# Attention and a maxout layer on one core: batch 1's second product stage in seven block products, with its weights' sums made earlier

## The chip, the cores and the metric

The kernel runs on one core of a Trainium2 chip. The core has a matrix engine (TensorE, "PE" in the profile, with its weight loads as "PEld"), a vector engine (VectorE, "DVE"), a scalar engine (ScalarE, "ACT"), a third elementwise engine (GpSimd, "POOL") and a queue engine that issues transfers (SyncE, "SP"). Each works through its own list of instructions in order, and they wait for each other through semaphores. The metric is the time in microseconds (us) of one execution on the device.

## The reference

Causal attention in a window of 128 for 8 batches, 8 heads, 576 rows and 64 columns a head, with a bias linear in distance, and then a layer that takes the largest of three products and multiplies it by an output matrix:

```python
scores = np.where(mask, scale * q @ k.T + bias, -1e9)      # mask: 0 <= rel < 128
attn   = softmax(scores)                                   # per head
x      = (attn @ v) with the heads side by side            # 4608 x 512
h      = np.maximum(np.maximum(x @ w1, x @ w2), x @ w3)    # 512 -> 768
out    = h @ w_out                                         # 768 -> 512
```

Everything is 32-bit. The kernel makes an exact-enough product from three products on PE: each operand is cut into a high part and a remainder, and high by remainder, remainder by high and high by high are summed in one bank of PSUM.

## The kernel before

The eight batches go one behind the other. Work on a batch has an attention part (L430 scores, L459 and L471 the softmax, L490 its division, L498 turns, L518 and L522 masks on POOL, L565 products with v, L598/599 the sums into `xk`) and then two stages of the layer, which take most of PE's time. Stage 1 makes nine groups of 128 rows of `h`, each from `x` and one of w1, w2, w3; stage 2 makes four groups of 128 rows of the output from `h`.

Each product of matrices is done on 2 by 2 blocks. In batches 0 and 1 ("plain", L773) it has eight block products, in two halves: stage 2 takes eight blocks of 18 matmuls, 144 in all. From batch 2 on (L825) it is done with seven block products, which need differences of the blocks on both sides: stage 2 takes 14 units of 9 matmuls, 126 in all. On the side of the weights the differences (called sums here) are made once; on the side of the data they are made per batch, by `factors_h` for stage 2: DVE makes four differences (L616), and seven factors are cut, each by an ACT cast (L612) and a DVE subtraction (L613). The plain way cuts four blocks and makes no difference.

The seven products of a group are added up in three banks of PSUM. The units come in the order k = 0, 1, 6, 2, 3, 4, 5, where k = 6 belongs to the group before. Unit 2 adds to the bank that unit 0 began, so it waits until unit 0's result has been copied out by ACT (L842); unit 3 does the same with unit 1's bank. At a plain stage there are only whole blocks, each begins a bank of its own, and three banks go round.

Weights' sums are made in the background, during batch 1 and the beginning of batch 2 (`more_sums`, called once for each unit of the layer): a load from DRAM by SP (`load_sums`, L230), four additions on POOL for each group (`sums`, L194, 128x256 each), a cut by two ACT casts (L199) and two DVE subtractions (L202), and a store by SP (`store_sums`). Groups 0 to 8 are stage 1's weights, and go back to DRAM, from where POOL's queue loads them into a ring for each batch (L361, L366). Groups 9 to 11 are stage 2's weights and stay on the chip in `ow`. They share one pair of buffers (`hs2`), each holding the rows of two groups. Before, groups are taken in the order 0 to 11.

A list of events with times sets the order of the program. PE's list is fixed by it; the other engines' lists are put in order by a scheduler, which places each instruction where its own model of time has it ready. SP's and POOL's transfers stand where the program has them. The order of each engine is shown below where it matters.

## Time and profile before

| | us |
|---|---|
| median of three runs (756.89 to 758.78) | 757.24 |
| the profiled execution | 755.7 |
| its span, first to last instruction | 754.0 |
| PE busy in it | 735.8 |
| DVE busy | 516.1 |
| ACT busy | 481.5 |
| POOL busy | 235.2 |

The granted clock of PE is at its upper level (1.0) over nearly the whole span. Times of instructions below count from the first instruction, so they are compared with the span; the execution's own time lies 1.7 us above it. Batch 1's layer begins at 161 us, its second stage at 235 us, and batch 2's layer at about 258 us.

### The profile page before, as it was taken

The numbers are of one execution on the slowest core, as the hardware profiler recorded it, in microseconds if no ns is written. First come the engines' busy times: TensorE is split into PE (matmuls) and PEld (weight loads), VectorE is DVE, ScalarE is ACT, GpSimd is POOL, SyncE is SP. The second block draws the span as 40 slices with busy tenths as digits, with TensorE's granted clock in tenths as the row PEclk, the third lists the DMA queues.
The fourth block names the chain that finished last, engine by engine and source line by source line (L and its number), as shares of the span: only waits on it lengthen the run. The fifth ranks groups of instructions, "written<-read, shape, count | busy, mean of one in ns | idle before, by whom it ended". The sixth has DMA issues, their size and how long they took to land.

```text
span 754.0 us, 19290 instructions
## 1 busy us (share of the span) xinstructions
PE 735.8 (98%) x7216; PEld 674.7 (89%) x7221; DVE 516.1 (68%) x1617; ACT 481.5 (64%) x1597; POOL 235.2 (31%) x451
## 2 busy tenths in 40 slices
PE   7979998999999999999999999999999999999998
PEld 3448897999999999999999999999999999999998
DVE  5869977636659567785678667794777747683663
ACT  5775677666667767776766757676666766552342
POOL 4651215545557123312222123221222122343100
PEclk9999999999999999999999999999999999999999
DMA  7867899759999289855988378864997468889711
GB/s 251 308 233 280 299 357 328 259 191 337 350 348 316 91 289 298 279 198 172 318 301 283 128 256 300 302 216 146 306 309 263 155 236 279 266 264 356 238 62 63
DMA packets 57085, 192.81 MB, mean 256 GB/s; under 512 B 5792, under 2 KB 24480, under 8 KB 50464
## 3 DMA queue, kind: packets, MB, share of 16 engines
q0 software_dynamic: 20304, 108.54, 43.3%
q1 hardware_dynamic: 36400, 82.85, 31.2%
q8 instruction: 57, 0.93, 0.5%
q14 instruction: 36, 0.29, 0.1%
q10 hardware_dynamic: 288, 0.20, 0.1%
HBM read 156.95 MB, written 34.60 MB: 254 GB/s over the span
## 4 chain that ended last, share of the span: by engine, by line
PE 77%; DVE 11%; ACT 6%; POOL 3%; issue 3%; DVEq 0%; ACTq 0%; POOLq 0%
PE ps_m L825 45%; PE ps_m L773 17%; PE ps_s L430 5%; PE ps_x L565 4%; PE pt L498 4%; DVE hs L613 2%; ACT p L471 2%; DVE hq L730 2%; DVE t L729 2%; POOL p L485 1%; ACT p L490 1%; POOL pp L522 1%; PE pt L374 1%; DVE t L616 1%; POOL pp L518 1%
## 5 line engine op out<-in xcount | busy, mean ns | idle before, releaser
L825 PE MATMUL ps_m<-xs,ring 128*128 128x288 f32 x2160 | 302.7, 297 | 0.6
L825 PEld LDWEIGHTS ps_m<-xs,ring 128*128 128x128 f32 x2160 | 290.1, 188 | 3.7 <-ACT t L842 3.2
L518 POOL TENSOR_SCALAR_AFFINE_SELECT pp<-pr 128x256 f32<-128x256 f32 x112 | 52.1, 465 | 281.4 <-ACT pr L502 155.8
L471 ACT ACTIVATE p<-s,st 128x128 f32<-128x128 f32 x288 | 114.7, 401 | 24.8 <-DVE st L459 22.6
L773 PE MATMUL ps_m<-xs,ring 128*128 128x288 f32 x864 | 122.5, 298 | 0.9 <-DVE hq L787 0.5
L842 ACT COPY t<-ps_m 128x288 f32<-128x288 f32 x196 | 76.7, 393 | 71.7 <-PE ps_m L825 69.7
L773 PEld LDWEIGHTS ps_m<-xs,ring 128*128 128x128 f32 x864 | 116.0, 188 | 3.6 <-issue 1.7
L366 POOL DMA_DIRECT2D ring<-keep x103 | 55.3, 537 | 166.0 <-PE ps_m L825 158.3
L825 PE MATMUL ps_m<-hs,ow 128*128 128x288 f32 x756 | 105.8, 297 | 0.4
L825 PEld LDWEIGHTS ps_m<-hs,ow 128*128 128x128 f32 x756 | 100.9, 188 | 2.7 <-ACT t L842 1.2
L490 ACT ACTIVATE p<-p,st 128x128 f32<-128x128 f32 x252 | 84.5, 393 | 22.2 <-DVE st L478 22.2
L729 DVE TENSOR_TENSOR t<-ps_m,t 128x288 f32<-128x288 f32 x108 | 48.8, 452 | 42.9 <-PE ps_m L825 32.5
L459 DVE CUSTOM_DVE_ANT_0 s<-ps_s,bias 128x128 f32<-128x128 f32 x240 | 60.9, 285 | 11.9 <-POOL bias L119 4.7
L430 PE MATMUL ps_s<-qk 64*64 64x192 f32 (+1 forms) x1088 | 61.4, 317 | 2.0 <-DVE st L459 1.3
L612 ACT CAST hs<-hq 128x288 fp32r<-128x288 f32 x96 | 40.4, 432 | 33.4 <-DVE hq L730 17.7
L471 ACT ACTIVATION_READ_ACCUMULATOR p<-s,st 128x1 f32 x288 | 55.3, 192 | 0.0
L565 PE MATMUL ps_x<-pp,v 64*64 64x64 f32 (+3 forms) x1456 | 53.4, 274 | 0.6 <-POOL pp L518 0.4
L498 PE MATMUL pt<-plus,p 128*128 128x128 f32 x288 | 48.7, 287 | 4.9 <-POOL p L485 4.4
L498 PEld LDWEIGHTS pt<-plus,p 128*128 128x128 f32 x288 | 30.4, 140 | 24.3 <-issue 11.5
L565 PEld LDWEIGHTS ps_x<-pp,v 64*64 64x64 f32 x1456 | 41.7, 133 | 11.0 <-issue 8.9
L730 DVE TENSOR_TENSOR hq<-t,hq 128x288 f32<-128x288 f32 x108 | 48.8, 456 | 2.1
L599 DVE TENSOR_TENSOR xk<-ps_x,xk 128x256 f32<-128x256 f32 (+3 forms) x56 | 25.4, 453 | 36.1 <-ACT xk L598 36.1
(92 smaller groups left out, 953.6 us busy)
## 6 DMA issues: line engine op xcount, KB each, us to landing
ring<-keep POOLq DMA_DIRECT2D x51, 1024.0 KB, 7.4
ring<-keep POOLq DMA_DIRECT2D x61, 768.0 KB, 6.0
qk<-in_qk SPq DMA_DIRECT2D x31, 576.0 KB, 5.6
hs<-in_w_all SPq DMA_DIRECT2D x12, 1023.6 KB, 7.0
v<-in_v SPq DMA_DIRECT2D x32, 320.0 KB, 6.6
outT<-t SPq DMA_DIRECT2D x64, 144.0 KB, 1.8
keep<-ring SPq DMA_DIRECT2D x9, 768.0 KB, 7.0
plain<-hs SPq DMA_DIRECT2D x12, 512.0 KB, 4.5
```

Source lines behind the costliest of these rows:

```text
L430: pe(nc.tensor.matmul(ps[j][d:d + D, o:o + k1 - k0], lhsT=qkt[u][j * D:(j + 1) * D, 0, q0:q0 + D], rhs=qkt[u][j * D:(j + 1) * D, 1, k0:k1] ...
L459: nc.vector.tensor_tensor_reduce(out=x, in0=ps[j][:, P:2 * P], in1=below, scale=-0.125, scalar=3.0e38, op0=ALU.add, op1=ALU.min, accum_out ...
L471: nc.scalar.activation(p[:, j], x, AF.Exp, bias=st[:, 0, a, j:j + 1], scale=-1.0, accum_out=st[:, 1, a, j:j + 1])
L490: nc.scalar.activation(p[:, j], p[:, j], AF.Copy, scale=st[:, 2, a, j:j + 1])
L498: pe(nc.tensor.transpose(out=pt[:, a, j], in_=p[:, j], identity=ident))
L518: nc.gpsimd.affine_select(out=old, in_=src, pattern=[[-x, n] for x, n in pat], compare_op=ALU.is_gt, fill=0.0, base=0, channel_multiplier=1,)
L565: pe(nc.tensor.matmul(x[j * D:(j + 1) * D, r, o:o + rhs.shape[1]], lhsT=vv[k, i, j * D:(j + 1) * D], rhs=rhs[k], start=start, stop=True, s ...
L729: nc.vector.tensor_tensor(out=s, in0=ps, in1=e, op=ALU.add)
L730: nc.vector.tensor_tensor(out=h, in0=s, in1=h, op=ALU.max)
L773: pe(nc.tensor.matmul(ps, lhsT=lt, rhs=rt, start=n == 0, stop=n == len(pairs) - 1, skip_group_check=True))
L825: pe(nc.tensor.matmul(part_of[n, {2: 0, 5: 0, 6: 0, 3: 1}.get(kk, kk)], lhsT=lt, rhs=rt, start=first, stop=i == len(pairs) - 1, skip_group ...
L842: nc.scalar.copy(out=e, in_=ps)
```

## The change

Batch 1's second stage takes seven block products, as the later batches do: the plain blocks of that stage are left out, and units 140 to 153 of the list take their place, 9 matmuls each (the last group's k = 6 follows in batch 2). For it, `factors_h` runs in batch 1's stage 1, and stage 1's last blocks come in the order (1,0), (0,0), (1,1), (0,1). The sums of stage 2's weights have to be there earlier, so groups 9, 10 and 11 come third to fifth; groups 7 and 8 come last, are loaded one at a time, and not before unit 156, that is, in batch 2. A group that is loaded alone uses the other half of its buffer for the high parts. The times after which a cut or a store may come are shortened by a unit.

```diff
--- before.py
+++ after.py
@@ -219,14 +219,18 @@
 
     now, loaded, finished = 0, 0, set()
     ts, to_sum, to_split = {}, [], []
+    sums_order = [0, 1, 9, 10, 11, 2, 3, 4, 5, 6, 7, 8]
 
     def load_sums():
         nonlocal loaded
         r = raw_tile()
-        for n in range(2):
-            g = loaded
+        single = loaded >= NG - 2
+        for n in range(1 if single else 2):
+            g = sums_order[loaded]
             loaded += 1
             ts[g] = t = r[:, 2 * DM * n:2 * DM * (n + 1)].rearrange("p (e w) -> p e w", e=4)
+            if single:
+                his[g] = r[:, 2 * DM:4 * DM].bitcast(F32R).rearrange("p (e w) -> p e w", e=4)
             nc.sync.dma_start(t.bitcast(F32), plain_keep[g])
             to_sum.extend((g, n, now + 8) for n in range(2))
 
@@ -238,7 +242,7 @@
             k, e = (slice(6, 7), slice(3, 4)) if a else (slice(1, 4), slice(0, 3))
             f = ow[:, k, g - 9]
             return hi_lo(f[:, :, 0], f[:, :, 1], t[:, e].bitcast(F32), True)
-        if a == 0:
+        if g not in his:
             x = xs_p.tile([P, 2, 2, C], F32R, name="xs")
             his[g] = x.rearrange("p a k c -> p (a k c)")[:, :2 * DM].rearrange("p (e w) -> p e w", e=4)
         e = slice(2 * a, 2 * a + 2)
@@ -251,8 +255,9 @@
         finished.add(g)
 
     def more_sums():
-        if loaded < NG and all(g in finished for g in range(loaded - 4, loaded - 2) if g >= 0):
-            load_sums()
+        if loaded < NG and all(g in finished for g in sums_order[max(0, loaded - 4):max(0, loaded - 2)]):
+            if loaded < NG - 2 or now >= 77 * PB + 2:
+                load_sums()
         if now < 63:
             return
         if to_split and now >= to_split[0][2] and (to_split[0][0] >= 9 or streamed > 2 * to_split[0][0] + 1):
@@ -260,14 +265,14 @@
             split_sums(g, a)
             if a:
                 if g < 9:
-                    later(now + 3, store_sums, g)
+                    later(now + 2, store_sums, g)
                 else:
                     finished.add(g)
         elif to_sum and now >= to_sum[0][2]:
             g, n, _ = to_sum.pop(0)
             sums(ts[g].bitcast(F32), n)
             if n:
-                to_split.extend((g, a, max(now + 6, 77 * PB if a and g >= 9 else 0)) for a in range(2))
+                to_split.extend((g, a, max(now + 5, 78 if a and g >= 9 else 0)) for a in range(2))
                 to_split.sort(key=lambda x: x[2])
 
     def place(n, a):
@@ -753,7 +758,7 @@
         if b == 0 and v == 1:
             spin(10)
         g, r = divmod(v, 4)
-        j, i = divmod(r, 2)
+        j, i = ((0, 0), (0, 1), (1, 0), (1, 1))[r] if b < PB - 1 else ((1, 0), (0, 0), (1, 1), (0, 1))[r]
         ps = ps_m.tile([P, 512], F32, name=f"ps_m{((PLAIN + 8) * b + v) % 3}")[:, :C]
         at = 9 * b + g
         if g < 9:
@@ -785,8 +790,10 @@
             return
         h = hq[p, (i, j)]
         nc.vector.tensor_tensor(out=h, in0=ps, in1=h, op=ALU.max)
-        if w == 2:
+        if w == 2 and b < PB - 1:
             later(unit_of(b, v + 1), plain_h, b, p, (i, j))
+        elif w == 2:
+            factors_h(b, p, (i, j), unit_of(b, v + 1))
 
     def unit(u):
         nonlocal now
@@ -795,7 +802,7 @@
         n, r = divmod(u, 7)
         k = (0, 1, 6, 2, 3, 4, 5)[r]
         n -= k == 6
-        if n < 11 * PB or n >= 11 * B:
+        if n < 11 * PB - 2 or n >= 11 * B:
             return
         if n == 11 * B - 1 and r > 4:
             k = 9 - k
@@ -830,7 +837,7 @@
         if g < 9:
             used.add((at, k))
         stream()
-        if b == PB and len(finished) < NG:
+        if len(finished) < NG:
             more_sums()
         if n == 11 * B - 2 and k < 2:
             for j in range(2 * k):
@@ -890,8 +897,13 @@
                     at(when, plain_x, b + 1)
                 else:
                     at(when, factors_x, b + 1, 77 * b + 63, 1.2)
-            at(when, plain, b, c)
-            when += pace if c < PLAIN else O_PACE * 14 / 8
+            if c < PLAIN or b < PB - 1:
+                at(when, plain, b, c)
+                when += pace if c < PLAIN else O_PACE * 14 / 8
+        if b == PB - 1:
+            for u in range(77 * b + 63, 77 * b + 77):
+                at(when, unit, u)
+                when += O_PACE
     for b in range(PB, B):
         pace = (ready[b + 1] - when) / 63 if b + 1 < B else O_PACE
         for u in range(77 * b, 77 * b + 77):
```

Three places show how instructions move.

On ACT, at the beginning of batch 1's layer (`hq<-ps_m` are copies of the first blocks out of PSUM, `xs<-hs` and `ow<-hs` casts of the sums), before:

```order
L199 CAST xs<-hs_1755 128x512 [waits DMAHW1_49,Pool_49]
L784 COPY hq<-ps_m_2339 128x288 [waits PE_49]
L490 ACTIVATE p<-p,st 128x128 [waits DVE_49]
L490 ACTIVATE p<-p,st 128x128 x3
L784 COPY hq<-ps_m_2364 128x288 [waits PE_49]
L199 CAST xs<-hs_1755 128x512
L199 CAST xs<-hs_1755 128x512 [waits DMAHW4_49,DMAHW5_49,DMAHW2_49,Pool_49]
L784 COPY hq<-ps_m_2392 128x288 [waits PE_49]
```

and in the changed kernel:

```order
L199 CAST ow<-hs_1755 128x256 [waits DMAHW1_49,Pool_49]
L495 ACTIVATE p<-p,st 128x128 [waits DVE_49]
L789 COPY hq<-ps_m_2343 128x288 [waits PE_49]
L495 ACTIVATE p<-p,st 128x128 x3
L199 CAST ow<-hs_1755 128x3x256 [waits DMAHW2_49,Pool_49]
L789 COPY hq<-ps_m_2367 128x288 [waits PE_49]
L199 CAST ow<-hs_1755 128x256
L789 COPY hq<-ps_m_2392 128x288 [waits PE_49]
L199 CAST ow<-hs_1755 128x3x256
```

The casts there are of stage 2's weights now, and the third of the copies (`ps_m_2367`) stands behind the cast of group 10's sums, which waits for POOL.

On POOL at the same place, before:

```order
L518 AFFINE_SELECT pp<-pr 128x2x128 [waits PE_49,Activation_49]
L522 AFFINE_SELECT pp<-pr 128x2x128 [waits PE_49]
L194 TENSOR_TENSOR hs_1755<-hs_1755 128x256 [waits DMAHW5_49,DMAHW1_49]
L194 TENSOR_TENSOR hs_1755<-hs_1755 128x256 [waits Pool_49]
L518 AFFINE_SELECT pp<-pr 128x2x128 [waits Activation_49]
L522 AFFINE_SELECT pp<-pr 128x2x128 [waits PE_49]
L518 AFFINE_SELECT pp<-pr 128x2x128
L522 AFFINE_SELECT pp<-pr 128x2x128 [waits PE_49]
L194 TENSOR_TENSOR hs_1755<-hs_1755 128x256 [waits Pool_49] x2
L194 TENSOR_TENSOR hs_1755<-hs_1755 128x256 [waits DMAHW2_49]
L194 TENSOR_TENSOR hs_1755<-hs_1755 128x256 [waits Pool_49]
L361 DMA ring<-keep_0_126 128x512 [waits DMASW0_49,PE_49]
```

and in the changed kernel:

```order
L523 AFFINE_SELECT pp<-pr 128x2x128 [waits Activation_49]
L527 AFFINE_SELECT pp<-pr 128x2x128 [waits PE_49]
L523 AFFINE_SELECT pp<-pr 128x2x128
L527 AFFINE_SELECT pp<-pr 128x2x128 [waits PE_49]
L194 TENSOR_TENSOR hs_1755<-hs_1755 128x256 [waits DMAHW5_49,DMAHW1_49]
L194 TENSOR_TENSOR hs_1755<-hs_1755 128x256 [waits Pool_49] x3
L194 TENSOR_TENSOR hs_1755<-hs_1755 128x256 [waits DMAHW2_49]
L366 DMA ring<-keep_0_126 128x512 [waits DMASW0_49,PE_49]
L194 TENSOR_TENSOR hs_1755<-hs_1755 128x256 [waits Pool_49] x3
```

The masks (AFFINE_SELECT) that stood between the sums come ahead of all of them, so eight additions and a ring load come in one piece.

On ACT, where batch 1's second stage begins (`hs` are factors of `h`, `xs` of `x`, `t<-ps_m` the copies of units 0, 1 and 2 or of a plain block), before:

```order
L490 ACTIVATE p<-p,st 128x128 x3
L612 CAST xs<-xt 128x576 [waits DMAHW6_49,DMAHW5_49,DVE_49]
L612 CAST hs<-hq 128x288 [waits DVE_49] x2
L598 COPY xk_3019<-ps_x 128x448 [waits PE_49]
L507 COPY pp<-pt 128x2x128 [waits PE_49,Pool_49]
L510 COPY pr<-pt 128x256
L612 CAST xs<-xt 128x576 [waits DVE_49]
L471 ACTIVATE p,st<-s,st 128x128 [waits DVE_49] x3
L713 COPY t<-ps_m_3481 128x288 [waits PE_49]
L471 ACTIVATE p,st<-s,st 128x128 [waits DVE_49]
```

and in the changed kernel:

```order
L617 CAST hs_3407<-hq 128x288 [waits DMAHW6_49,DMAHW3_49,DMAHW7_49,DMAHW2_49,DVE_49]
L617 CAST xs<-xt 128x576 [waits DMAHW7_49,DMAHW5_49]
L617 CAST hs_3407<-t_3399 128x288 [waits DVE_49]
L617 CAST hs_3407<-hq 128x288 [waits DVE_49]
L617 CAST hs_3407<-t_3400 128x288 [waits DVE_49]
L617 CAST hs_3496<-hq 128x288 [waits DMAHW4_49,DMAHW1_49,DMAHW5_49,DMAHW0_49,DVE_49]
L617 CAST hs_3496<-hq 128x288 [waits DVE_49]
L603 COPY xk_3026<-ps_x 128x448 [waits PE_49]
L617 CAST hs_3496<-t_3400 128x288 [waits DVE_49]
L512 COPY pp<-pt 128x2x128 [waits PE_49,Pool_49]
L515 COPY pr<-pt 128x256
L617 CAST xs<-xt 128x576 [waits DMAHW3_49,DMAHW2_49,DVE_49]
L849 COPY t<-ps_m_3504 128x288 [waits PE_49]
```

Seven casts of `h` and two of `x`, the second of which waits for DVE, stand ahead of the first copy of a unit's bank.

On PE at that place in the changed kernel (before, four blocks of 18 matmuls stood here, each in a bank of its own):

```order
L832 MATMUL ps_m_3504<-hs,ow 128x288 [waits DVE_49]
L832 MATMUL ps_m_3504<-hs,ow 128x288 x5
L832 MATMUL ps_m_3504<-hs_3407,ow 128x288 [waits DVE_49]
L832 MATMUL ps_m_3504<-hs_3407,ow 128x288 [waits Activation_49]
L832 MATMUL ps_m_3504<-hs_3407,ow 128x288
L832 MATMUL ps_m_3522<-hs,ow 128x288 [waits DVE_49]
L832 MATMUL ps_m_3522<-hs,ow 128x288 x5
L832 MATMUL ps_m_3522<-hs_3407,ow 128x288 [waits DVE_49]
L832 MATMUL ps_m_3522<-hs_3407,ow 128x288 [waits Activation_49]
L832 MATMUL ps_m_3522<-hs_3407,ow 128x288
L832 MATMUL ps_m_3504<-hs,ow 128x288 [waits Activation_49]
L832 MATMUL ps_m_3504<-hs,ow 128x288 x5
```

The third unit begins in the bank of the first (`ps_m_3504`), with a wait for ACT.

On POOL, in batch 2's first stage, before:

```order
L366 DMA ring<-keep_1_125 128x1536 [waits DMASW3_49,PE_49]
L366 DMA ring<-keep_0_126 128x2048 [waits DMASW5_49,PE_49]
L366 DMA ring<-keep_1_127 128x1536 [waits DMASW4_49,PE_49]
L518 AFFINE_SELECT pp<-pr 128x2x128 [waits Activation_49]
L522 AFFINE_SELECT pp<-pr 128x2x128 [waits PE_49,Pool_49]
L366 DMA ring<-keep_0_128 128x2048 [waits DMASW6_49,PE_49]
L366 DMA ring<-keep_1_129 128x1536 [waits DMAHW5_49,DMASW7_49,PE_49]
L366 DMA ring<-keep_0_130 128x2048 [waits DMASW0_49,PE_49]
```

and in the changed kernel:

```order
L371 DMA ring<-keep_1_125 128x1536 [waits DMAHW5_49,DMASW3_49,PE_49]
L194 TENSOR_TENSOR hs_3825<-hs_3825 128x256 [waits DMAHW4_49,DMAHW6_49,DMAHW3_49,DMAHW7_49,DMAHW2_49,DVE_49]
L371 DMA ring<-keep_0_126 128x2048 [waits DMASW5_49,PE_49]
L194 TENSOR_TENSOR hs_3825<-hs_3825 128x256 [waits Pool_49]
L371 DMA ring<-keep_1_127 128x1536 [waits DMAHW5_49,DMASW4_49,PE_49]
L194 TENSOR_TENSOR hs_3825<-hs_3825 128x256 [waits Pool_49] x2
L194 TENSOR_TENSOR hs_3840<-hs_3840 128x256 [waits DMAHW1_49,DMAHW5_49,DMAHW0_49,DVE_49]
L194 TENSOR_TENSOR hs_3840<-hs_3840 128x256 [waits Pool_49] x3
L371 DMA ring<-keep_0_128 128x2048 [waits DMASW6_49,PE_49]
L523 AFFINE_SELECT pp<-pr 128x2x128 [waits Activation_49]
```

The eight additions of groups 7 and 8 now stand between the loads of the ring.

## Rows read from the trace of the kernel before

**Rows 1.** the page, busy time of each engine: us, share of the span

```profile
PE 735.8 (98%) x7216; PEld 674.7 (89%) x7221; DVE 516.1 (68%) x1617; ACT 481.5 (64%) x1597; POOL 235.2 (31%) x451
```

**Rows 2.** windows of before, busy us of each engine in 20 us, then clock

```profile
220.00:240.00 20.00, 20.00 (x214) 19.18 (x213) 15.08 (x44) 13.94 (x47) 15.18 (x24) 1.00 1.00 334
240.00:260.00 20.00, 20.00 (x192) 19.20 (x191) 13.35 (x34) 14.82 (x47) 7.33 (x11) 1.00 0.42 146
```

**Rows 3.** list of waits from 140 us on: total us, times, longest

```profile
PEld ps_m L825 <- ACT t L842: 4.4, 16, 0.3
```

**Rows 4.** timeline of PE round batch 1's second stage: start us, us, line

```profile
226.69 6.62 PE L773 MATMUL ps_m<-xs,ring 128*128 128x288 f32 x48
...
235.35 9.69 PE L773 MATMUL ps_m<-hs,ow 128*128 128x288 f32 x72
...
246.19 9.77 PE L773 MATMUL ps_m<-hs,ow 128*128 128x288 f32 x72
```

**Rows 5.** timeline of POOL, 164 to 168 us

```profile
164.20 3.52 POOL L194 TENSOR_TENSOR hs<-hs 128x256 f32<-128x256 f32 x4
167.67 0.57 POOL L361 DMA_DIRECT2D ring<-keep  x1
```

**Rows 6.** one line's instructions, L194 on POOL: ns min/median/max, first and last start

```profile
L194 POOL TENSOR_TENSOR hs<-hs x48: 724/742/1251, 138.8 to 244.1; 128x256 f32<-128x256 f32 x48
```

**Rows 7.** timeline of ACT across the seam, 238 to 243 us

```profile
238.23 0.67 ACT L612 CAST xs<-xt 128x576 fp32r<-128x576 f32 x1 [1.88 <-DVE xt L616]
...
239.97 0.38 ACT L713 COPY t<-ps_m 128x288 f32<-128x288 f32 x1
...
242.65 0.83 ACT L199 CAST ow<-hs 128x768 fp32r<-128x768 f32 x1
```

**Rows 8.** timeline of ACT, 167 to 171 us

```profile
170.38 0.39 ACT L784 COPY hq<-ps_m 128x288 f32<-128x288 f32 x1
```

**Rows 9.** timeline of PE, 161 to 178 us

```profile
171.39 6.63 PE L773 MATMUL ps_m<-xs,ring 128*128 128x288 f32 x48
```

**Rows 10.** timeline of POOL, 238 to 278 us

```profile
238.44 6.79 POOL L194 TENSOR_TENSOR hs<-hs 128x256 f32<-128x256 f32 x6
...
273.19 0.53 POOL L366 DMA_DIRECT2D ring<-keep  x1 [3.35 <-PE ps_m L825]
...
277.12 0.55 POOL L366 DMA_DIRECT2D ring<-keep  x1
```

**Rows 11.** timeline of DVE across the seam, 231 to 245 us

```profile
233.72 0.81 DVE L787 TENSOR_TENSOR hq<-ps_m,hq 128x288 f32<-128x288 f32 x2
...
236.46 0.61 DVE L599 TENSOR_TENSOR xk<-ps_x,xk 128x448 f32<-128x448 f32 x1
...
237.32 0.87 DVE L616 TENSOR_TENSOR xt<-xk,xt 128x576 f32<-128x576 f32 x1
...
241.35 3.29 DVE L613 TENSOR_TENSOR xs<-xk,xs 128x576 fp32r<-128x576 f32 x3 [0.34 <-ACT xs L612]
```

**Rows 12.** one line's instructions, L613 on DVE, 250 to 400 us: ns min/median/max

```profile
L613 DVE TENSOR_TENSOR xs<-xk,xs x5: 742/745/853, 316.9 to 335.5; 128x576 fp32r<-128x576 f32 x5
```

**Rows 13.** groups of DVE and ACT instructions by form: busy us, mean ns

```profile
L613 DVE TENSOR_TENSOR hs<-hq,hs 128x288 fp32r<-128x288 f32 x96 | 44.1, 473 | 5.9 <-ACT hs L612 5.7
```

**Rows 14.** timeline of PE, PEld and ACT at the seam from batch 2 to 3

```profile
322.65 2.61 PE L825 MATMUL ps_m<-hs,ow 128*128 128x288 f32 x18
326.10 4.75 PEld L825 LDWEIGHTS ps_m<-hs,ow 128*128 128x128 f32 x36 [0.29 <-ACT t L842]
325.68 0.37 ACT L842 COPY t<-ps_m 128x288 f32<-128x288 f32 x1
```

**Rows 15.** DMA issues by form: KB each, median us from issue to landing

```profile
ring<-keep POOLq DMA_DIRECT2D x51, 1024.0 KB, 7.4
...
keep<-hs SPq DMA_DIRECT2D x9, 384.0 KB, 6.4
```

**Rows 16.** timeline of PE in batch 2

```profile
284.76 7.67 PE L825 MATMUL ps_m<-xs,ring 128*128 128x288 f32 x54
```

## The prediction

> **What bounds the kernel now.** I read the busy times first: PE is busy for 735.8 of 754.0 us, 98% [rows 1]. The windows say whether that holds at the place of the change: between 220 and 260 us PE is busy in all of it, at a granted clock of 1.00, with DVE at 13 to 15 us and ACT at 14 to 15 us in 20 [rows 2]. The list of waits then shows what little PE waits for: from 140 us on only the weight loads of the seven-product stages, which wait for ACT's copies 16 times, 4.4 us together and 0.3 at most [rows 3]. So fewer matmuls are worth their full time there, but only as long as the other engines keep PE supplied; there is no idle time of PE to give back, and each wait that the change makes is a loss of its own length. A measurement of this kernel can tell a change of about 0.3%, 2.3 us, from none.
>
> **What is removed.** Batch 1's second stage has 144 matmuls before (eight blocks of 18) and 126 afterwards (14 units of 9). The 72 matmuls of its first half take 9.69 us, those of the second 9.77 [rows 4]; by starts and ends that is 0.1346 us each, so 18 fewer give 18 x 0.1346 = 2.42 us. The last 9 of the 126 come in batch 2, which changes nothing in the sum. The gain as a whole is thus 0.32%, hardly more than a measurement can see, and every wait that is added counts against it.
>
> **Term A, the beginning of batch 1's layer.** The sums of groups 9 and 10 are made here in one piece: eight additions and a ring load on POOL, behind masks that end at 164.20 us. Four additions there take 3.52 us and the ring load's issue 0.57 [rows 5], so the piece takes between 8 x 0.742 + 0.57 = 6.5 us (by the median of the line [rows 6]) and 8 x 0.88 + 0.57 = 7.6: it ends between 170.7 and 171.8. ACT's cast of 128x768 waits for the last addition (0.83 us in [rows 7]), and the copy of `ps_m_2367` is queued behind it; the same copy ran at 170.38 at the latest before [rows 8]. With 0.05 us to start, some 0.75 for the cast and 0.39 for the copy, the bank is free between 171.9 and 173.0. PE wants it with the first matmul at 171.39 [rows 9]. That is a wait of 0.5 to 1.6 us; I take 1.0. The same pattern comes once more with group 11, whose additions have a ring load's issue in front of them: nothing to 0.57 us by that issue, taken as 0.3 (term B).
>
> Under these sums lies a question of contention. The additions on POOL take 742 ns in the median but 1251 at the most [rows 6]. Six of them beside large subtractions of DVE took 6.79 us, 1.13 each [rows 10], and three of these subtractions took 3.29 us, 1.10 each [rows 11], where the same form takes 0.745 when no additions run [rows 12]. So an addition and a subtraction cost each other about 0.35 us where they meet. The Trainium skill (SBUF — State Buffer, section "Who interferes with whom") states more: a VectorE operation with two SBUF inputs and a GpSimd operation that reads SBUF shut each other out for the whole operation. By that rule eight additions could hold DVE for 8 x 0.742 = 5.9 us; by the rows it is 8 x 0.35 = 2.8. The trace agrees in direction, and the price that I use is that of the rows.
>
> **Term C, the seam into batch 1's second stage.** This is the largest term. Unit 2 begins in unit 0's bank, so it waits for ACT's first copy. Units 0 and 1 are 18 matmuls, from 235.35 us to 235.35 + 2.42 = 237.77; that is when PE wants the copy. ACT has seven casts of `h` and two of `x` ahead of it, and the second cast of `x` waits for DVE's subtraction into `xt`. DVE's list is counted from the third block's maximum. Stage 1's last four blocks end 1.65 us apart, the last at 233.31 [rows 4], so that maximum runs from 231.75 to 232.15. Then come, at 0.4 us from start to start (two maxima take 0.81 us [rows 11]; a cut's subtraction is 0.473 in the mean [rows 13]): a subtraction of `x` (0.7), five operations of 288 columns, to 234.85; the last maximum and three more, 1.6; the sum into `xk`, 0.5 net of 0.61; one more cut, 0.4; a masked copy, 0.4; and the `xt` subtraction, 0.87 [rows 11]. That ends at about 238.6. Before, the same `xt` subtraction started at 237.32 and its cast on ACT waited 1.88 us for it and ran at 238.23, and the first copy at 239.97 [rows 7]; that hurt nothing, because plain blocks use three banks in turn. Now the cast begins at 238.65, the copy at about 239.35, and it ends at 239.75: PE waits 2.0 us.
>
> The nearest rows for a bound are those of a seam that has this form already. There PE begins at 322.65, the first copy starts at 325.68, 3.03 later, and six matmuls of unit k = 6 lie between, so that the wait is 0.29 [rows 14]. The copy's end there is 3.4 us behind the start of unit 0; without these six matmuls, as here, the wait would be 3.4 - 2.42 = 1.0. So C lies between 1.0 and, with DVE 0.5 us later, 2.5. Below nothing it can't be, since PE doesn't wait there now.
>
> What follows in that stage (two casts between the second copy and unit 3, the outputs' additions on DVE instead of copies on ACT) I cost at nothing: the wait at unit 2 lets ACT and DVE catch up. The buffers that the casts write were the sums' before, and SP's stores have to be done with them; a store takes 6.4 us in the median [rows 15] and is issued some 7 to 8 us ahead, so it is hidden by about 1 us, and if it isn't it takes part in the same wait.
>
> **Term D, batch 2's first stage.** The eight additions of groups 7 and 8 stand between ring loads on POOL. Six of them come behind the load that PE releases, 273.19 + 0.53 = 273.72 [rows 10]; at 0.86 each that is 278.9, where the next load of 1 MB was issued at 277.12 before [rows 10]. It lands 7.4 us later in the median [rows 15], at 286.3, and PE wants it six matmuls into the group that starts at 284.76, at 285.57 [rows 16]: 0.7 us late. With additions at 0.742 it is issued at 278.2 and lands in time; with 1.13 it is issued at 280.5 and is 2.3 us late. I take 0.7, from nothing to 2.3.
>
> **The sum.** -2.42 + 1.0 (A) + 0.3 (B) + 2.0 (C) + 0.7 (D) = +1.6 us on the profiled execution's 755.7, so 757.3 there. The median of the three runs shown is 757.24, 1.5 above the profiled one; a difference carries over, and the forecast is 757.24 + 1.6 = 758.8 us.
>
> **Rivals.**
>
> 1. Everything is hidden, and the gain shows in full: 757.24 - 2.42 = 754.8. For it: ACT and DVE idle for 32 and 36% of the span [rows 1], and the scheduler placed the copy where its own model of time had it ready. Against it: the order of ACT and DVE above leaves no room for the copy before 237.77. Slightly faster, at the edge of what can be seen.
> 2. The seam costs only what the regular one would (1.0), A its lower end (0.5), B and D nothing: 757.24 - 2.42 + 1.5 = 756.3. For it: the regular seam is measured, and my count of DVE's list is worth 0.5 us either way. Against it: the regular seam has fewer operations of DVE between.
> 3. Slower: POOL's additions in batch 2 run beside DVE's subtractions and take 1.13 us each, as they did at 238 us [rows 10]. The price is D's upper end of 2.3 from the late ring load, so 757.24 - 2.42 + 1.0 + 0.3 + 2.0 + 2.3 = 760.4, and up to 6 x 0.35 = 2.1 more, 762.5, if what DVE loses by it shows in PE's waits for banks. It decides against the change from the point where the load is issued after 285.57 - 7.4 = 278.2. For it: stage 1 of batch 2 has subtractions in it of the same sort. Against it: the median is 742 ns [rows 6], and DVE is less busy there than at the seam. The rule of the skill named above speaks for this case.
>
> **How the numbers follow.** The forecast's case has 0.34, and its own range, from the lower and upper ends of C and of half of A, is 757.5 to 759.7. Rival 1 has 0.21, rival 2 0.20, rival 3 0.25. Faster by over 0.3% (below 754.97) is rival 1, with 0.01 from rival 2: 0.22. Slower (above 759.5) is rival 3 and a quarter of the forecast's case: 0.33. The rest, 0.45, is within 0.3%. The range that leaves out 2 in 10 goes from rival 1's time, 754.8, to just below rival 3's upper price, 762.0.
>
> **What would show it.** In the changed profile the second stage of batch 1 should show 14 units of L832 where eight blocks of L773 stood. If C is right, the weight loads of L832 wait for ACT's copy once for about 2 us near 238 us, and that is the longest of PE's waits; if rival 2 is, for about 1; if rival 1 is, not at all. A shows as a wait of L778 for ACT's copy near 171 us, behind a cast that waits for POOL's L194; D as a wait of a weight load of batch 2's stage 1 for the ring near 285 us. The forecast is wrong if the windows from 160 to 300 us show PE busy in full as before, or if waits of more than 1 us show in places that are not named here, above all behind unit 3 in the second stage or at SP's stores.

## The result, and the profile after

| | before | changed |
|---|---|---|
| median | 756.89 us (5 runs, 755.21 to 758.78) | 766.55 us (5 runs, 765.42 to 768.58) |
| profiled execution | 755.7 | 768.58 |
| ratio | | 1.0131, interval 1.0114 to 1.0148 |

The change makes the kernel 1.3% slower, 9.7 us, well outside the range of the prediction. The page of the changed kernel, busy time of each engine, against [rows 1]:

```profile
PE 739.9 (96%) x7198; PEld 674.8 (88%) x7203; DVE 527.3 (69%) x1644; ACT 484.5 (63%) x1606; POOL 234.2 (31%) x451
```

DVE is busy for 11.2 us more, ACT for 3.0, PE for 4.1 although it has 18 matmuls less (its granted clock fell twice in this execution, as shown below). In the kernel before, PE's matmuls waited for nothing from 130 us on. In the changed kernel they have these waits (who waits for whom, us in total, times, longest):

```profile
PE ps_m L778 <- DVE hq L792: 2.2, 3, 1.4
PE ps_m L832 <- ACT t L849: 2.1, 1, 2.1
PE ps_m L832 <- DVE t L734: 1.9, 2, 1.1
PE ps_m L778 <- ACT hq L789: 1.2, 3, 0.8
PE ps_m L832 <- DMA ring<-keep: 0.6, 1, 0.6
```

Together that is 8.0 us. Four of the five are waits in the places of terms A and B (L778, stage 1 of batch 1) and D (L832 for DVE and for the ring); only the 2.1 us are at the seam. The timeline of PE shows where they stand (start, us, engine, line, count, idle time before it):

```profile
174.61 5.06 PE L778 MATMUL ps_m<-xs,ring 128*128 128x288 f32 x36 [0.17 <-ACT hq L789]
179.95 1.86 PE L778 MATMUL ps_m<-xs,ring 128*128 128x288 f32 x12 [0.27 <-DVE hq L792]
...
199.63 1.86 PE L778 MATMUL ps_m<-xs,ring 128*128 128x288 f32 x12 [0.81 <-ACT hq L789]
...
220.55 1.86 PE L778 MATMUL ps_m<-xs,ring 128*128 128x288 f32 x12 [1.42 <-DVE hq L792]
...
243.11 2.61 PE L832 MATMUL ps_m<-hs,ow 128*128 128x288 f32 x18
247.77 6.55 PE L832 MATMUL ps_m<-hs,ow 128*128 128x288 f32 x36 [2.06 <-ACT t L849]
...
288.49 1.07 PE L832 MATMUL ps_m<-xs,ring 128*128 128x288 f32 x6 [0.74 <-DVE t L734]
290.70 4.26 PE L832 MATMUL ps_m<-xs,ring 128*128 128x288 f32 x30 [1.15 <-DVE t L734]
...
298.33 6.91 PE L832 MATMUL ps_m<-xs,ring 128*128 128x288 f32 x48 [0.61 <-DMA ring<-keep]
```

PE's list is the same in both kernels but for the second stage. So its time can be taken apart by the distance from one group of products with v (L565 before, L570 now) to the next, from the timelines of the profiled executions:

| stretch (times of before) | before | changed | lost |
|---|---|---|---|
| 169.5 to 178.0 (term A) | 8.44 | 9.42 | 0.98 |
| 178.0 to 225.0 (term B) | 47.08 | 51.04 | 3.96 |
| 225.0 to 264.4 (second stage, with the nine matmuls in batch 2) | 39.32 | 40.82 | 1.50, where -2.42 was due: 3.92 |
| 264.4 to 301.7 (term D) | 37.35 | 40.91 | 3.56 |

Together that is 10.0 us; from 302 us to the end the two kernels agree within 0.1 us. The profiled execution also lost 2.8 us before 140 us, where PE's granted clock fell to 0.50 between 15 and 20 us. PE's list there is the same in both kernels, and the profiled execution without additions (below) does not lose it, so I count it to that one execution, which was 2.0 us above the median.

The seam, answering to [rows 7, 11], in ACT's and DVE's timelines:

```profile
246.75 0.67 ACT L617 CAST xs<-xt 128x576 fp32r<-128x576 f32 x1 [1.25 <-DVE xt L621]
247.33 0.39 ACT L849 COPY t<-ps_m 128x288 f32<-128x288 f32 x1
```

```profile
245.97 0.75 DVE L621 TENSOR_TENSOR xt<-xk,xt 128x576 f32<-128x576 f32 x1
```

The copy is behind the cast, and the cast behind the `xt` subtraction, as forecast; PE's wait is 2.06 us. What was not forecast stands in the next view, the windows round it (span; busy us and counts of PE, PEld, DVE, ACT, POOL; granted clock; DMA share; GB/s):

```profile
244.00:248.00 4.00, 1.94 (x15) 1.71 (x14) 3.90 (x14) 2.75 (x9) 1.36 (x2) 1.00 1.04 394
248.00:252.00 4.00, 4.00 (x22) 4.00 (x22) 2.30 (x7) 3.67 (x14) 0.00 (x0) 0.63 0.36 146
```

PE had stood still for two of four microseconds, and then the granted clock was 0.63 in the mean of the next four: the lower of the two levels (0.5) for most of it. The 36 matmuls behind the wait took 6.55 us; where the clock stayed up (below) they took 5.04.

### The profile page after: what moved, and what is told of

The parts are those of the page before. It is cut to its first block, busy times and chain, and to the rows that moved or that the text cites. A ratio compares the mean times of both kernels' runs of the same rounds, so it can differ in the third digit from the quotient of the medians.

```text
span 766.9 us, 19313 instructions
## 1 busy us (share of the span) xinstructions
PE 739.9 (96%) x7198; PEld 674.8 (88%) x7203; DVE 527.3 (69%) x1644; ACT 484.5 (63%) x1606; POOL 234.2 (31%) x451
## 4 chain that ended last, share of the span: by engine, by line
PE 64%; DVE 14%; ACT 8%; POOL 5%; DMA 3%; issue 3%; SPq 0%; DVEq 0%; ACTq 0%; POOLq 0%
PE ps_m L832 46%; PE ps_m L778 7%; PE ps_s L435 4%; PE pt L503 3%; PE ps_x L570 3%; DVE hs L618 3%; ACT p L476 2%; POOL hs L194 2%; DVE hq L735 2%; DVE t L734 2%; ACT p L495 1%; DVE t L621 1%; DMA qk<-in_qk 1%; DMA ring<-keep 1%; POOL pp L527 1%
## 5 line engine op out<-in xcount | busy, mean ns | idle before, releaser
L832 PE MATMUL ps_m<-xs,ring 128*128 128x288 f32 x2160 | 303.9, 297 | 3.2 <-DVE t L734 1.9
L832 PEld LDWEIGHTS ps_m<-xs,ring 128*128 128x128 f32 x2160 | 290.2, 188 | 7.3 <-ACT t L849 3.2
L476 ACT ACTIVATE p<-s,st 128x128 f32<-128x128 f32 x288 | 114.8, 401 | 25.5 <-DVE st L464 24.1
L778 PE MATMUL ps_m<-xs,ring 128*128 128x288 f32 x864 | 123.9, 299 | 4.3 <-DVE hq L792 2.7
L832 PE MATMUL ps_m<-hs,ow 128*128 128x288 f32 x882 | 124.9, 299 | 2.5 <-ACT t L849 2.1
L849 ACT COPY t<-ps_m 128x288 f32<-128x288 f32 x202 | 78.8, 393 | 75.1 <-PE ps_m L832 73.2
L832 PEld LDWEIGHTS ps_m<-hs,ow 128*128 128x128 f32 x882 | 119.3, 190 | 4.9 <-ACT t L849 3.5
L778 PEld LDWEIGHTS ps_m<-xs,ring 128*128 128x128 f32 x864 | 116.1, 188 | 8.4 <-DVE hq L792 3.5
L464 DVE CUSTOM_DVE_ANT_0 s<-ps_s,bias 128x128 f32<-128x128 f32 x240 | 61.0, 285 | 11.5 <-POOL bias L119 4.6
L476 ACT ACTIVATION_READ_ACCUMULATOR p<-s,st 128x1 f32 x288 | 55.4, 192 | 0.0
L570 PE MATMUL ps_x<-pp,v 64*64 64x64 f32 (+3 forms) x1456 | 53.5, 274 | 0.6 <-POOL pp L523 0.4
L735 DVE TENSOR_TENSOR hq<-t,hq 128x288 f32<-128x288 f32 x108 | 50.4, 471 | 2.1
L570 PEld LDWEIGHTS ps_x<-pp,v 64*64 64x64 f32 x1456 | 41.7, 133 | 11.0 <-issue 8.9
```

What stands on the lines that cost most here:

```text
L464: nc.vector.tensor_tensor_reduce(out=x, in0=ps[j][:, P:2 * P], in1=below, scale=-0.125, scalar=3.0e38, op0=ALU.add, op1=ALU.min, accum_out ...
L476: nc.scalar.activation(p[:, j], x, AF.Exp, bias=st[:, 0, a, j:j + 1], scale=-1.0, accum_out=st[:, 1, a, j:j + 1])
L570: pe(nc.tensor.matmul(x[j * D:(j + 1) * D, r, o:o + rhs.shape[1]], lhsT=vv[k, i, j * D:(j + 1) * D], rhs=rhs[k], start=start, stop=True, s ...
L735: nc.vector.tensor_tensor(out=h, in0=s, in1=h, op=ALU.max)
L778: pe(nc.tensor.matmul(ps, lhsT=lt, rhs=rt, start=n == 0, stop=n == len(pairs) - 1, skip_group_check=True))
L832: pe(nc.tensor.matmul(part_of[n, {2: 0, 5: 0, 6: 0, 3: 1}.get(kk, kk)], lhsT=lt, rhs=rt, start=first, stop=i == len(pairs) - 1, skip_group ...
```

## The experiments

All times are medians, and "less" is against the changed kernel's 766.55 us; the kernel before ran beside each set. Of each edit the lines that matter are shown, "..." marks where some are left out. The scheduler orders ACT's and DVE's lists anew for each edit, so these lists are not quite the same from run to run. The first question was which of two things made B and D so large: the extra work on factors, or POOL's additions.

**No additions.** `sums(ts[g], n)` is left out, so the sums are the plain blocks.

```diff
-            sums(ts[g].bitcast(F32), n)
```

> The changed kernel without POOL's additions of the background sums (L194), all of them; loads, casts, subtractions and stores stay. In the changed kernel's trace 4.0 us were lost between 193 and 234 us (waits for ACT's and DVE's maxima and copies), 1.0 at 172 us, 4.0 net at the second stage's start and 3.6 between 285 and 307 us. If the additions matter only where PE's wait comes behind them, the 1.0 at 172 us and the 3.6 in batch 2 go, and the rest stays: about 762. The rival is that additions and subtractions shut each other out all through batch 1, and that the 4.0 us come from that as well: then about 758. If they matter nowhere, 766.6.

It took 757.69 us (before beside it 756.65; ratio 1.0014, 0.9996 to 1.0032), 8.9 less than the changed kernel: the rival came true. Its page, and two of the three waits of PE from 130 us on (the third is 0.2 us):

```profile
PE 734.2 (97%) x7198; PEld 672.5 (89%) x7203; DVE 518.9 (69%) x1644; ACT 483.9 (64%) x1606; POOL 195.4 (26%) x403
```

```profile
PE ps_m L831 <- ACT t L848: 1.2, 1, 1.2
PE ps_m L831 <- DVE hq L734: 0.3, 1, 0.3
```

All waits of batch 1's stage 1 are gone, the distances there are those of before to 0.01 us (8.44, 10.07, 8.55, 9.96, 8.54, 9.97), and DVE, with the same instructions, is busy for 518.9 us instead of 527.3. The wait at the seam is 1.2 instead of 2.1, and batch 2's first stage still loses 0.7 us against before.

**Four cuts.** `factors_h` in batch 1 cuts the four blocks and makes no difference; units 4 to 6 read the factors of 0 to 2, so stage 2 of batch 1 is not the product. The additions stay.

```diff
...
+        if b < PB:
+            ks = {(0, 1): (3,), (0, 0): (0,), (1, 1): (2,), (1, 0): (1,)}[ij]
+            for k in ks:
+                later(when, cut, k, hq[p, ij])
...
```

> The changed kernel with four factors of h cut in batch 1 instead of seven, and without their four differences (units 4, 5 and 6 read the factors of 0, 1 and 2); PE's list is the same. If DVE's and ACT's extra work on factors makes the maxima late, the 4.0 us between 193 and 234 us go, and the wait for the first copy at the seam shrinks below 1 us, so that the clock does not fall: between 758.5 and 761. The rival, that the waits come from the sums in the background, gives 766 with at most the seam better (763).

It took 762.25 us, 4.3 less. PE's waits (one of 0.2 us is left out):

```profile
PE ps_m L844 <- DVE t L746: 2.7, 3, 1.2
PE ps_m L790 <- DVE hq L804: 0.6, 2, 0.3
PE ps_m L844 <- ACT t L861: 0.2, 1, 0.2
```

The wait at the seam is down to 0.2 us, and B to 0.6 us in one stretch (9.15 where before has 8.55). A stays (9.42), and batch 2 loses 5.0 us here instead of 3.56, because the clock fell there (0.8 between 280 and 288 us). So B needs both: it goes without the additions, and nearly goes without the extra work on factors.

**Filling the wait at the seam.** 16 matmuls into a bank of the turns, ahead of the unit that waits.

```diff
+        if u == 77 * (PB - 1) + 63 + 3:
+            fill = ps_t.tile([P, 512], F32, name="pt")[:, :C]
+            for i in range(16):
+                _, lt, rt = pairs[0]
+                pe(nc.tensor.matmul(fill, lhsT=lt, rhs=rt, start=i == 0, stop=i == 15, skip_group_check=True))
```

> The changed kernel with 16 more matmuls (2.15 us) on PE ahead of the unit that waits 2.06 us for the first copy, into a bank of the turns that nobody reads. If the granted clock falls because PE stands still there, and the 36 matmuls behind it took 6.55 instead of 4.98 us for that reason, the clock stays at 1.00 near 250 us and the time falls by about 1.6 us, to 765.0. If these matmuls were slow for another reason, the time stays at 766.6 or rises a little.

It took 767.27 us (four runs, 765.09 to 770.10): no gain. In its profiled execution the clock stayed up at the seam and fell later, in batch 2, behind D's waits (windows, clock third from the end):

```profile
248.00:252.00 4.00, 3.87 (x30) 3.64 (x29) 3.12 (x8) 3.43 (x12) 0.00 (x0) 1.00 0.34 141
280.00:300.00 20.00, 18.11 (x182) 16.72 (x183) 16.59 (x46) 12.85 (x41) 9.59 (x16) 0.91 1.02 353
```

So the fall is not tied to this one wait; by this one execution, filling moves it at most.

**The cuts of x later.** They are due four units later than in the changed kernel.

```diff
-                    at(when, factors_x, b + 1, 77 * b + 63, 1.2)
+                    at(when, factors_x, b + 1, 77 * b + 67, 1.2)
```

> The changed kernel with the cuts of batch 2's x due four units later, so that no cast of x stands ahead of the first copies on ACT. By the theory that the copy was late by ACT's order, PE's wait at the seam falls from 2.06 us to 0.5 or less, the clock stays up, and the time falls by 3 to 3.6 us, to 763. The rival is that the same work is late a moment later, at the first units of batch 2, which need these factors: then the wait moves there and the time stays within 1 us of 766.6.

It took 765.50 us, 1.0 less, which the intervals do not tell from the changed kernel (ratio 1.0088 to 1.0136 against 1.0114 to 1.0148), and the mechanism was missed. The wait is still 2.06 us, as PE's timeline shows, with ACT's behind it:

```profile
246.73 5.04 PE L832 MATMUL ps_m<-hs,ow 128*128 128x288 f32 x36 [2.06 <-ACT t L849]
```

```profile
241.96 0.77 ACT L617 CAST hs<-hq 128x288 fp32r<-128x288 f32 x2 [0.83 <-DMA keep<-hs]
...
245.51 0.40 ACT L476 ACTIVATE p<-s,st 128x128 f32<-128x128 f32 x1 [0.82 <-DVE st L464]
...
246.30 0.38 ACT L849 COPY t<-ps_m 128x288 f32<-128x288 f32 x1
```

With the casts of `x` away, the scheduler put the softmax's L476 ahead of the copy, and that waits for DVE too; before that, ACT's casts of `h` had waited 0.83 us for a store of the sums. The queue's next item took the place of the one removed. The 36 matmuls took 5.04 us here at a clock of 1.00: the same wait, without the fall.

**Memsets for additions.** Each addition is replaced by three memsets of the same piece, so the sums are zeros; they occupy POOL but read nothing.

```diff
+MEMSETS = 3
...
-            tc.keep_in_program_order(nc.gpsimd.tensor_tensor(out=t[:, to], in0=t[:, a], in1=t[:, b], op=op))
+            for _ in range(MEMSETS):
+                tc.keep_in_program_order(nc.gpsimd.memset(t[:, to], 0.0))
```

> The changed kernel with each of POOL's additions replaced by three memsets of the same 128x256 piece, which read nothing from SBUF (so the sums are zeros); POOL stays occupied and ACT's casts still wait for it. Without the additions the time fell to 757.7. If the additions hurt because their reads and DVE's subtractions shut each other out, the memsets do not hurt DVE: DVE's subtractions of 128x288 stay at 0.45 us and the waits between 193 and 234 us and near 290 us are gone, the wait near 172 us (ACT behind POOL) may stay: 757.5 to 759.5. If it is POOL's occupancy (casts and ring loads queued behind it), the time stays near 766.

It took 759.87 us (ratio to before 1.0030, 1.0013 to 1.0048), just above the range expected if the reads were what hurts. POOL's line (ns min/median/max):

```profile
L196 POOL MEMSET hs<- x144: 301/314/341, 140.1 to 290.6; 128x256 f32 x144
```

POOL is busy as long as in the changed kernel (233.9 against 234.2 us), and yet DVE is back at 518.8 us and stage 1 of batch 1 at before's distances (8.44, 10.07, 8.54, 9.96, 8.72, 9.96). DVE's subtractions of 128x288 take 0.46 us at most there (1.98 in the changed kernel, between 160 and 235 us). DVE's list is the same in stage 1 but for a few instructions that stand a place or two elsewhere. So what stretches DVE's instructions is not POOL's being busy but what its additions read. How much of B is this stretching is not shown by it: ACT's casts of the sums, too, wait less for POOL here (4.8 us in all between 160 and 306 us, 11.5 in the changed kernel), and some of them stand a few places later in ACT's list. For A this run proves still less: the copy stands ahead of the cast there. In batch 2, 1.1 us of waits for the ring remain (loads behind POOL's pieces), with 2.1 us lost between 264 and 302 us.

**Without the additions of groups 7 and 8**, the ones in batch 2, alone:

```diff
-            sums(ts[g].bitcast(F32), n)
+            if g not in (7, 8):
+                sums(ts[g].bitcast(F32), n)
```

> The changed kernel without the additions of groups 7 and 8 alone, the ones that stand in batch 2. By the reading of the trace they cost what batch 2's stage 1 lost between 275 and 307 us, 3.3 us less the 0.7 that stayed without any additions: the time falls by 2.6 us, to 764, and the waits between 193 and 234 us stay as they are. The rival, that batch 2's loss follows from the late second stage of batch 1 and not from its own additions, gives 766.5.

It took 762.64 us, 3.9 less where 2.6 was expected. Batch 2's loss falls from 3.56 to 1.1 us, and the rest of the difference is the clock, which did not fall at the seam in the profiled execution (the 36 matmuls behind the same wait took 4.99 us). B and A stay to 0.02 us. So the eight additions cost 2.5 us of D. The meeting is part of it: in the changed kernel DVE's subtractions of 128x512 there took 964 ns in the mean, here 680. It is not all of it, because memsets, which read nothing, left 2.1 us of loss there.

**Unit 4 third**, which puts 1.2 us between unit 1 and unit 2:

```diff
-        k = (0, 1, 6, 2, 3, 4, 5)[r]
+        k = ((0, 1, 6, 4, 2, 3, 5) if n == 11 * PB - 2 else (0, 1, 6, 2, 3, 4, 5))[r]
```

> The changed kernel with batch 1's first group in the order of units 0, 1, 4, 2, 3, 5: unit 4 begins a bank of its own and puts 9 matmuls (1.21 us) between unit 1 and unit 2, which waits for the copy. The wait of 2.06 us at the seam becomes 0.85, the second stage no longer lets PE stand still for 2 us, and the time falls by 1.2 us, or by up to 2.8 where the granted clock had fallen behind the wait: 764.5 at the middle. The rival: unit 4's own factor, the last one that is cut, is late, or a later unit waits instead, and the time stays at 766.5.

It took 764.86 us, 1.7 less, with the whole result; by the intervals that is no clear difference (1.0070 to 1.0124 against 1.0114 to 1.0148). The wait became 0.89, as expected, and unit 5 then waits 0.64:

```profile
241.84 3.79 PE L832 MATMUL ps_m<-hs,ow 128*128 128x288 f32 x27
246.51 2.63 PE L832 MATMUL ps_m<-hs,ow 128*128 128x288 f32 x18 [0.89 <-ACT t L849]
249.79 1.45 PE L832 MATMUL ps_m<-hs,ow 128*128 128x288 f32 x9 [0.64 <-ACT t L849]
```

In the profiled executions the stretch from the second stage to batch 2's first group takes 38.93 us, against 39.27 in the run with the cuts of `x` later, which has the old order and no fall of the clock either. So the order alone shows as 0.3 us; the rest of the 1.7 goes with the clock.

**No additions and unit 4 third.** This run has the edits of "No additions" and of "Unit 4 third" together.

> No additions at all and the unit order 0, 1, 4, 2, 3, 5 together. Without additions PE still waited 1.18 us at the seam; the unit order should take that away. If nothing else is in the way, the 18 matmuls now show: 757.7 less 1.2, 756.5, that is 0.3 below the kernel before, with 0.7 us still lost in batch 2's stage 1. If the gain of 2.4 us comes out whole it is 754.5; if the wait only moves on, it stays at 757.7.

It took 757.25 us (ratio 1.0010, 0.9995 to 1.0025), between the first and the last of its three expectations: one wait of 0.6 us is left at the seam, and 0.7 us for the ring in batch 2.

**Additions on DVE**, with unit 4 third, the whole result:

```diff
-            tc.keep_in_program_order(nc.gpsimd.tensor_tensor(out=t[:, to], in0=t[:, a], in1=t[:, b], op=op))
+            tc.keep_in_program_order(nc.vector.tensor_tensor(out=t[:, to], in0=t[:, a], in1=t[:, b], op=op))
```

> The unit order 0, 1, 4, 2, 3, 5 of the run before, with the additions made by DVE instead of POOL; it computes the whole result. Additions and subtractions then stand in one queue and cannot meet, ACT waits for no POOL, and the ring loads have nothing ahead of them; but DVE gets 48 additions of some 0.42 us, 20 us more work, where the meeting of the two cost DVE 8.4 us. By the theory that the meeting is what costs, it is faster than with POOL (764.9): about 760. If what counts is only how much DVE has to do in batch 1, it is slower: 768 or more.

It took 758.05 us (before beside it 757.67; ratio 1.0000, 0.9978 to 1.0023). The additions on DVE, and PE's waits from 130 us on:

```profile
L194 DVE TENSOR_TENSOR hs<-hs x48: 393/419/658, 141.4 to 273.3; 128x256 f32<-128x256 f32 x48
```

```profile
PE ps_m L832 <- DMA ring<-keep: 1.4, 1, 1.4
PE ps_m L832 <- ACT t L849: 1.2, 2, 0.6
```

DVE is busy for 535.4 us here, 8.1 more than in the changed kernel, and PE waits for 2.6 us in all instead of 8.0. Batch 1's stage 1 is at before's distances in all six stretches. That settles the rival "DVE has too much to do" for A and B. D is only in part better: batch 2's first stage still loses 2.0 us, 1.4 of them in the wait for the ring.

**The kernel before without the additions**, by the same edit as in "No additions", is the other corner:

> The kernel before without the additions of the background sums. If the additions cost time only together with the changed kernel's extra work on factors, since before PE waited for nothing from 140 us on, the time stays as before within 0.3%: 756 to 758. If they cost PE something in the kernel before too, it falls below 755.

It took 756.14 us against 757.67 beside it (ratio 0.9975, 0.9953 to 0.9997): 1.5 us less at the middle of an interval that begins at 0.2. In its trace the distances from 137 us on are before's to 0.07 us, and the first addition starts at 138.8 us. So the additions cost 8.9 us in the changed kernel, and by the medians 1.5 in the one before, which no wait or stretch of PE shows; where these would come from stays open. DVE is busy for 509.7 us here: the additions made its instructions 6.4 us longer in the kernel before as well (516.1), and the change's own work on DVE is 9.2 us (518.9 without additions).

**Sooner cuts and stores**, on top of additions on DVE and unit 4 third:

```diff
-                to_split.extend((g, a, max(now + 5, 78 if a and g >= 9 else 0)) for a in range(2))
+                to_split.extend((g, a, max(now + 2, 78 if a and g >= 9 else 0)) for a in range(2))
...
-                    later(now + 2, store_sums, g)
+                    later(now + 1, store_sums, g)
```

> The run before (additions on DVE, unit order 0, 1, 4, 2, 3, 5), with the sums' cuts due three units and the stores one unit sooner; the result is whole. In the run before PE still waited 1.2 us at the seam, where ACT's casts wait for a store of the sums, and 1.4 us near 294 us for a ring load that shares the DMA engines with the stores of the last two groups. If sooner stores take half of both away, the time falls by 1.2 us, to 756.8, at last below the kernel before (757.7) by some 0.1%. If the cuts on ACT and DVE only get in the way of other work, it stays at 758 or rises.

It took 763.62 us (before beside it 757.02), a miss. Its six runs lie between 759.35 and 765.08, and the one with a trace is the lowest: there 0.8 us is lost in batch 1's stage 1 again, and the waits at the seam are 1.8 in all. To what the other runs lost 3 to 6 us more, no trace shows; it stays open.

**Additions on DVE alone**, with the changed kernel's unit order:

> The changed kernel with one edit: the additions on DVE instead of POOL; the unit order is that of the changed kernel, and the result is whole. With both edits the time was 758.05, and the unit order alone was worth 1.7 us (766.55 to 764.86). If the meeting of additions and subtractions is the main cause, this one edit takes 7 us or more: 758.5 to 760. If the two edits worked only together, it stays above 763.

It took 759.56 us (ratio 1.0042, 1.0022 to 1.0061), 7.0 less than the changed kernel. The two longest of PE's waits:

```profile
PE ps_m L832 <- ACT t L849: 2.2, 1, 2.2
PE ps_m L832 <- DMA ring<-keep: 1.0, 1, 1.0
```

A and B are gone altogether (8.44 in A's stretch, and before's distances to 0.01 us in B's). The seam's wait stands as in the changed kernel, and the clock fell behind it here too (0.57 between 244 and 248 us; the 36 matmuls took 6.55 us). D is 1.6 us. No version of the changed kernel is faster than the kernel before: the best whole one is level with it.

## Why the prediction was wrong

The forecast was +1.6 us, and +9.7 came. Term by term:

- **The gain, right as far as it can be seen.** The 18 fewer matmuls were to give 2.42 us from the second stage to the first stretch of batch 2. In the run with four cuts, which waits least there (0.2 us), that stretch takes 37.53 us against 39.32, 1.8 less; some 0.4 us of the gain is not accounted for.
- **Term A, right in size, in part by luck.** It was 0.98 us against 1.0. The wait that was forecast, for the copy behind the cast that waits for POOL, is less than half of it: the first matmul came at 174.61 where the kernel before would have had it at 174.20 (171.39 [rows 9] and the 2.81 us by which the changed kernel is late here), so 0.4 us, below the range of 0.5 to 1.6. The other 0.6 is a wait for DVE's maximum (PE's row at 179.95 above). It was not forecast: DVE's list stood still for 6.81 us ahead of the subtraction that cuts the same sums and waits for ACT's casts of them, and the maximum behind it came late:

```profile
173.43 0.83 ACT L199 CAST ow<-hs 128x768 fp32r<-128x768 f32 x1 [3.42 <-POOL hs L194]
174.17 0.39 ACT L789 COPY hq<-ps_m 128x288 f32<-128x288 f32 x1
```

```profile
176.00 0.96 DVE L202 TENSOR_TENSOR ow<-hs,ow 128x768 fp32r<-128x768 f32 x1 [6.81 <-ACT ow L199]
...
179.44 0.45 DVE L792 TENSOR_TENSOR hq<-ps_m,hq 128x288 f32<-128x288 f32 x1
```

- **Term B, the step that failed.** It was taken as "the same pattern once more", one ring issue of 0.57 us at most, and priced at 0.3; the rest of stage 1 lost 3.96. The pattern itself cost nothing: ACT's casts of group 11's sums did wait 1.37 us for POOL, but the stretch in which they stand takes 10.07 us, as before:

```profile
188.39 1.14 ACT L199 CAST ow<-hs 128x768 fp32r<-128x768 f32 x2 [1.37 <-POOL hs L194]
```

The loss is in the four stretches behind it (1.07, 0.73, 1.67 and 0.48 us), which the forecast did not name; its own sign of being wrong, a wait of more than 1 us in an unnamed place, stands at 220.55 us. Two things were left out of its working. One is that stage 1 of batch 1, too, gets more work from the change: in the seam's count DVE's differences and extra cuts were all listed, but for the first two thirds of `h` they fall between 186 and 223 us, and nothing was reckoned there. The other is the meeting of additions and subtractions. [rows 6, 10, 11] had its price, about 0.35 us, and the forecast worked out 2.8 us for eight additions; but as a loss of DVE's time it stands in no term of the sum, and only in rival 3, for batch 2. The lines of the changed kernel round the longest of these waits, on POOL, DVE and ACT:

```profile
208.56 4.33 POOL L194 TENSOR_TENSOR hs<-hs 128x256 f32<-128x256 f32 x4
```

```profile
208.77 1.07 DVE L202 TENSOR_TENSOR hs<-hs,xs 128x512 fp32r<-128x512 f32 x1 [1.24 <-POOL pp L527]
...
220.04 0.45 DVE L792 TENSOR_TENSOR hq<-ps_m,hq 128x288 f32<-128x288 f32 x1
...
220.62 1.03 DVE L621 TENSOR_TENSOR t<-hq,t 128x288 f32<-128x288 f32 x1
221.57 0.99 DVE L618 TENSOR_TENSOR hs<-hq,hs 128x288 fp32r<-128x288 f32 x1
```

```profile
212.92 0.62 ACT L199 CAST xs<-hs 128x512 fp32r<-128x512 f32 x1 [1.84 <-POOL hs L194]
213.44 1.28 ACT L495 ACTIVATE p<-p,st 128x128 f32<-128x128 f32 x4
214.63 0.42 ACT L617 CAST hs<-hq 128x288 fp32r<-128x288 f32 x1
```

Four additions take 4.33 us instead of 2.97 (0.742 each [rows 6]). ACT's casts wait for them, and the softmax and the casts of `h` are queued behind these casts. DVE then has seven operations on factors and the scores to catch up with, one behind the other from 215.1 us on, and the maximum that frees PE's bank runs at 220.04 for a bank that PE wants at 219.1. (The two stretched rows behind it, beside the next six additions, show the meeting from DVE's side.) The memsets and the additions on DVE show where the chain begins: B is down to 0.2 us when POOL's instructions read nothing, and gone when DVE makes the additions. The four cuts show that the extra work on factors is needed too. The links between are read from this timeline and not tried one by one, and how B divides between DVE's longer instructions and ACT's waits for POOL stays open.

- **Term C, right in place and wait, wrong in its price.** The wait was 2.06 us against 2.0, in part by luck: without the additions it was 1.2, with the same order on ACT, and the count of DVE's list had no additions in it. So the count was some 0.8 too long, and the additions put 0.9 on top. A consequence was missing: with the clock at its lower level behind the wait the same 36 matmuls took 1.5 us more (6.55 against 5.04). The clock fell there in two profiled executions with this wait (the changed kernel, additions on DVE alone) and not in two others (the cuts of `x` later, no additions of groups 7 and 8); why, is open. The sentence that what follows costs nothing, since the wait lets ACT and DVE catch up, forgot PE. SP's stores were not quite hidden either: ACT's casts of `h` waited 0.4 us for one, ahead of the longer wait for DVE.
- **Term D, mis-sized.** 0.7 was taken from a range of 0 to 2.3, and 3.56 was measured; 0.7 stays without any additions. The mechanism of rival 3 was the right one, with both its parts, but in other shares: 1.9 us of waits for DVE, behind subtractions stretched to 1.13 us, and 0.6 for the ring:

```profile
283.31 5.35 POOL L194 TENSOR_TENSOR hs<-hs 128x256 f32<-128x256 f32 x6
```

```profile
285.81 2.26 DVE L202 TENSOR_TENSOR hs<-hs 128x512 fp32r<-128x512 f32 x2
```

The range ended at 762.0, because only one of its terms was ever put at its upper end, and because DVE's loss by the meeting was looked for in batch 2 alone. (Rival 1 also names the idle shares the wrong way round: by [rows 1] DVE is idle for 32% and ACT for 36%; nothing hangs on it.) As to where the meeting happens, the Trainium skill's rule (SBUF — State Buffer, section "Who interferes with whom") was the better guide: a VectorE instruction with two SBUF inputs contends with a GpSimd instruction that reads SBUF, and not with one that only writes it. The traces agree: DVE is busy for 518.8 us beside POOL's memsets, which read nothing, 518.9 beside no additions and 527.3 beside the additions; and the maxima L792, with one input in PSUM, take 0.46 us at most beside them. As to the price, DVE lost 0.18 us for each addition in the mean, less than the 0.35 of the rows.

## What to carry to other kernels

Background work on GpSimd is not free merely because GpSimd is idle: count how many of its instructions read SBUF beside VectorE instructions with two SBUF inputs, and ask how much slack VectorE has in that stage. In the kernel before, whose matmuls wait for nothing from 130 us on, the additions made VectorE's instructions 6.4 us longer and no stretch of PE showed it; with the change's 9.2 us of work on VectorE the same additions cost 8.9 us. So a new cost is to be looked for in every stage where the slack shrinks, and not only where instructions move. Where a cost is found by rows, it is to be put into every term in which the rows' condition holds. And a term that comes out right as a sum can still be wrong in its parts, as A and C were.

## What was not expected of the hardware

An addition of 128x256 takes 0.42 us on DVE and 0.74 on POOL in the median, and up to 1.34 on POOL beside DVE; a memset there takes 0.31. A subtraction of 128x288 on DVE takes 0.45 us in the median and took 1.98 once, beside POOL's additions:

```profile
187.39 1.98 DVE L618 TENSOR_TENSOR hs<-t,hs 128x288 fp32r<-128x288 f32 x1
```

The 48 additions on POOL made DVE's own instructions longer by 8.4 us in all (527.3 against 518.9), 0.18 for each addition, and cost the kernel 8.9. After PE had stood still for 2.1 to 2.2 us at the seam, the granted clock fell to its lower level in two profiled executions and stayed at 1.00 in two others; the 36 matmuls behind it took 6.55 us in both of the first and 5.04 and 4.99 in the others.
